# Attention in a fused kernel: 296 TensorE transposes of rounded keys and queries, issued as plain matmuls instead of in transpose mode

## Chip, core and metric

One core of one Trainium2 chip runs the whole program in one launch. The metric is the device time of that launch in microseconds (us), as the median of several runs; a profile of one further execution shows where the time goes.

## What is computed

The program chains an attention, a gated feed-forward layer and a layer of eight experts with two chosen per token. The change is in the attention alone:

```python
# q, k, v: (2, 8, 1152, 64) float32
q_pool = q.reshape(B, H, S // 2, 2, D).mean(axis=3)          # 576 pooled queries
scores = scale * np.matmul(q_pool, k.transpose(0, 1, 3, 2))  # 576 x 1152 a head
scores = scores - np.max(scores, axis=-1, keepdims=True)
attn = np.exp(scores)
attn = attn / (np.sum(attn, axis=-1, keepdims=True) + 1e-09)
out = np.matmul(attn, v)
x = out.transpose(0, 2, 1, 3).reshape(B * S // 2, H * D)     # 1152 tokens
# then: RMS norm, silu(x @ w_gate) * (x @ w_val) @ w_out; then the experts
```

## The kernel before

The attention works on two heads at a time, which makes eight pairs (`p`). Keys and pooled queries come in with tokens on the partitions. For a float32 result from TensorE's faster rounded type (F32R), each is split into a rounded part and the remainder: `khl` holds rounded keys and remainders side by side (9 chunks of 128 columns a head), `qh2` the rounded queries twice, `Ql` the queries' remainders, with the negated row maximum of the scores in one further column.

TensorE contracts over partitions, so all three are turned by transposes of 128x128 blocks: a block is the stationary operand (a weight load, engine PEld in the profile), the 128x128 unit matrix `identr` the moving one. `trans` (L131 to L143) collects up to four blocks in one PSUM bank `tt`, and ScalarE copies the bank out to `KT`, `QH` or `QlT`. `ql_trans2` (L175 to L181) does the same for four leftover blocks, one of them with a permuted unit matrix `swapr`.

For one pair there are six banks of four blocks, one of one and one of two (`kq_trans`), two banks of three (`ql_trans`) and one of four (`ql_trans2`): 37 blocks, 296 over the eight pairs.

The rest of a pair: `s1` (L188 to L191) makes scores for the row maximum, three matmuls of 384 columns a step, and VectorE reduces them (L193). `st_exp` makes the scores again, transposed and with the remainders added, by matmuls of 288 columns (L202, L203), and ScalarE takes the exponential (L204) into `et`. `avmm` (L229) multiplies `et` with the values in plain float32, and `sums` (L245) adds up the rows.

The order of the work is written out by hand: in pair `p` the lists `S_S1A`, `S_KA`, `S_QA` and so on put steps of the next pair (its transposes, most of its `s1`) between the 18 steps of `st_exp`. Every engine runs its own instructions in this order. The transposes of the first pair stand in a prologue before the loop, with those of `kq_trans` for the pairs 1 to 7 in the loop's periods 0 to 6.

A weight load can run while the matmul before it is still streaming; the load after that one has to wait until the matmul in between has started.

Of the kernel before, what the change touches and what calls it, by code (L numbers as in the profile page):

```python
# [9 lines left out]
F32 = mybir.dt.float32  # L10
F32R = mybir.dt.float32r
# [10 lines left out]
def fused_kernel(ctx, tc, q, k, v, w_gate, w_val, w_out, rms_g,  # L22
                 r_gate, r_noise, noise, e_w1, e_w2, out, dbg=None):
    nc = tc.nc
    P = 128
# [11 lines left out]
    pe, dve, act, pool, sp = nc.tensor, nc.vector, nc.scalar, nc.gpsimd, nc.sync  # L37
# [4 lines left out]
    identr = const.tile([P, P], F32R, name="identr")  # L42
# [43 lines left out]
    raw, khl, qh2, KT, QhT, QlT, V = {}, {}, {}, {}, {}, {}, {}  # L86
# [42 lines left out]
    tpool = [pst]  # L129

    def trans(srcs, evacs):  # L131
        t = tpool[0].tile([P, 512], F32R, name="tt", tag="T")
        tpool.append(tpool.pop(0))
        for i, a in enumerate(srcs):
            pe.transpose(t[:, i * P:(i + 1) * P], a, identr)
        for eng, o, lo, hi, rows in evacs:
            i = t[0:rows, lo:hi].bitcast(F32)
            if len(o.shape) == 3:
                i = i.rearrange("p (h c) -> p h c", h=2)
            if eng is act:  # L140
                act.copy(o, i)
            else:
                eng.tensor_copy(o, i)  # L143

    def kq_trans(p, h, i):
        if i == 0:
            KT[p, h] = ab.tile([P, S], F32R, name="KT", tag=f"KT{h}", bufs=NKT[h])
            qt = QH[p % 2].rearrange("p (h c) -> p h c", h=2)
            QhT[p, 0], QhT[p, 1], QhT[p] = qt[:, 0], qt[:, 1], qt
        kt = KT[p, h]  # L150
        kk = khl[p, h].rearrange("p c a d -> p c (a d)")
        qq = qh2[p, h].rearrange("p c a d -> p c (a d)")
        if i < 2:
            o = i * 512
            trans([kk[:, 4 * i + c] for c in range(4)], [(act, kt[:, o:o + 512], 0, 512, P)])
        elif i == 2:
            trans([qq[:, c] for c in range(4)], [(act, QhT[p, h][:, 0:512], 0, 512, P)])
        else:
            ev = [(act, kt[:, 1024:], 0, P, P)]
            if h == 0:  # L160
                trans([kk[:, 8]], ev)
            else:
                trans([kk[:, 8], qq[:, 4]], ev + [(act, QhT[p][:, :, QF:SQ], P, 2 * P, P),
                                                  (dve, QZ[p % 2][:, QR:], P + QR, 2 * P, P)])
# [8 lines left out]
        trans([Ql[p % 3][h][:, c] for c in range(3)], [(act, QlT[p, h][:, 0:384], 0, 384, P)])  # L173

    def ql_trans2(p):  # L175
        t = tpool[0].tile([P, 512], F32R, name="tt", tag="T")
        tpool.append(tpool.pop(0))
        for i, (a, m) in enumerate(((Ql[p % 3][0][:, 3], identr), (Ql[p % 3][1][:, 4], identr),
                                    (Ql[p % 3][1][:, 3], identr), (Ql[p % 3][1][:, 4], swapr))):
            pe.transpose(t[:, i * P:(i + 1) * P], a, m)  # L180
        act.copy(QlT[p][:, :, 384:], t.bitcast(F32).rearrange("p (h c) -> p h c", h=2)[:, :, 0:192])  # L181

    def s1(p, h, c):
        t = ps[0].tile([P, 3, 512], F32, name="s1", tag="s1", bufs=ps[1])
# [240 lines left out]
    for p in range(NPB):  # L425
# [19 lines left out]
        at(sl["s1b"][0], s1, p, 1, 3)  # L445
        at(sl["s1a"][1], s1, p, 1, 4)
        at(sl["qa"][0], ql_trans2, p)
        if p + 2 < NPB:
            if p == 0:
# [35 lines left out]
        for i in range(NST):  # L485
            g, c = divmod(i, KC)
# [1144 lines left out]
```

## Time and profile before

| | |
|---|---|
| median of 3 runs | 782.76 us (781.74 to 783.29) |
| profiled execution, its own time | 782.14 us |
| its span in the profile | 780.1 us |
| TensorE matmuls (PE) busy | 746.0 us, 96% of the span |
| weight loads (PEld) busy | 619.9 us, 79% |
| VectorE (DVE), ScalarE (ACT), GpSimd (POOL) busy | 525.2, 375.7, 258.5 us |

The attention runs until about 267 us, the feed-forward layer and the experts follow. A matmul's busy time counts its whole latency, so that overlapping matmuls can fill the PE row although TensorE waits a little in between: starts, one after another, say more than durations. PEclk, or the granted clock, is the share of full clock that the chip recorded for TensorE (1.00 is 2.4 GHz, 0.5 is 1.2 GHz).

### The profile page before, as it was taken

Reading aid. Unit: us, or ns where it says so; the run is one execution under the profiler, and the core shown is the slowest. Engines: PE = TensorE matmul, PEld = TensorE weight load, DVE = VectorE, ACT = ScalarE, POOL = GpSimd, SP = SyncE. Lnnn points to the kernel's source line nnn. Section 1 sums busy time; section 2 is a strip of 40 time slices with the busy share of each in tenths; the row PEclk is TensorE's granted clock in tenths of the full one; section 3 lists DMA queues with packets and bytes.
Section 4 is the critical chain, followed back from the end, with each engine's and each line's share of the span. In section 5 each row is a group of like instructions: output and inputs, shape, how many; then the busy total and the mean of one; then the engine's idle time right before and its main releaser. Section 6 shows DMA issues by size and latency. Waiting matters only on the chain. (4 is left out here: it accounts for less than half of the span.)

```text
span 780.1 us, 13462 instructions
## 1 busy us (share of the span) xinstructions
PE 746.0 (96%) x5102; PEld 619.9 (79%) x5102; DVE 525.2 (67%) x798; ACT 375.7 (48%) x766; POOL 258.5 (33%) x221
## 2 busy tenths in 40 slices
PE   5999999999999989999999999999999999999993
PEld 4877777877777668988888889988899898978762
DVE  6677777787779967576568654659856766748520
ACT  4665655665667553534233323355444455537510
POOL 8356365384813431122122310020323213422222
PEclk9999999999999999999999999999999999999997
DMA  7344232322041131133133201555898768879982
GB/s 224 90 134 139 83 85 53 107 77 61 27 134 63 56 108 55 55 108 108 55 108 109 57 1 55 183 180 193 280 358 258 229 186 251 271 228 361 354 263 61
DMA packets 72729, 113.29 MB, mean 145 GB/s; under 512 B 7127, under 2 KB 37551, under 8 KB 72656
## 3 DMA queue, kind: packets, MB, share of 16 engines
q1 hardware_dynamic: 67504, 101.55, 40.2%
q0 software_dynamic: 5152, 10.80, 6.3%
q8 instruction: 42, 0.69, 0.4%
q14 instruction: 31, 0.25, 0.1%
HBM read 98.16 MB, written 9.65 MB: 138 GB/s over the span
## 5 line engine op out<-in xcount | busy, mean ns | idle before, releaser
L536 PE MATMUL gv<-XN,ws 128*128 128x256 f32 (+2 forms) x912 | 165.2, 331 | 0.9 <-POOL ws L402 0.9
L536 PEld LDWEIGHTS gv<-XN,ws 128*128 128x128 f32 x912 | 143.8, 189 | 15.0 <-issue 1.8
L193 DVE TENSOR_REDUCE Ql<-s 128x1 fp32r<-128x1152 f32 x72 | 97.3, 1355 | 56.5 <-PE s L188 34.5
L204 ACT ACTIVATE et<-st 128x288 f32<-128x288 f32 x288 | 103.3, 417 | 40.9 <-PE st L203 38.6
L1086 DVE TENSOR_TENSOR wz<-raw,wz 128x1024 fp32r<-128x1024 f32 x80 | 96.0, 1222 | 28.9 <-ACT wz L106 26.4
L402 POOL TENSOR_TENSOR ws<-wm,ws 128x1024 fp32r<-128x1024 f32 x18 | 43.9, 2440 | 154.5 <-ACT ws L401 139.6
L202 PE MATMUL st<-QH,KT 128*128 128x288 f32 x288 | 91.8, 334 | 2.4 <-ACT et L204 1.0
L1187 PE MATMUL py<-wz,hTT 128*128 128x512 f32 x384 | 93.9, 395 | 0.0
L557 PE MATMUL po<-ws,hT 128*128 128x512 f32 x324 | 83.2, 395 | 2.2 <-DVE X L562 2.1
L203 PE MATMUL st<-QlT,KT 128*128 128x288 f32 x288 | 81.4, 296 | 0.0
L106 ACT CAST wz<-raw 128x1024 fp32r<-128x1024 f32 x80 | 81.1, 1047 | 0.4 <-PE py L1187 0.4
L1187 PEld LDWEIGHTS py<-wz,hTT 128*128 128x128 f32 x384 | 70.0, 188 | 13.7 <-DVE hTT L1055 0.2
L229 PE MATMUL av<-et,v 128*64 128x288 f32 x576 | 77.4, 412 | 0.5 <-ACT xT L234 0.5
L202 PEld LDWEIGHTS st<-QH,KT 128*128 128x128 f32 x288 | 54.5, 189 | 21.9 <-issue 12.3
L557 PEld LDWEIGHTS po<-ws,hT 128*128 128x128 f32 x324 | 58.9, 188 | 14.2 <-DVE X L562 3.3
L217 DVE TENSOR_TENSOR es<-es,et 128x576 f32<-128x576 f32 x64 | 62.3, 973 | 1.5
L1263 POOL DMA_INDIRECT out_dram<-yo,sidx x16 | 30.6, 1910 | 96.5 <-DVE yo L1262 55.8
L229 PEld LDWEIGHTS av<-et,v 128*64 128x64 f32 x576 | 38.3, 136 | 27.7 <-issue 3.9
L1160 PEld LDWEIGHTS ph<-xgT,wz 128*128 128x128 f32 x480 | 57.7, 189 | 0.4
L1160 PE MATMUL ph<-xgT,wz 128*128 128x256 f32 x480 | 57.8, 281 | 0.0
L203 PEld LDWEIGHTS st<-QlT,KT 128*128 128x128 f32 x288 | 54.8, 190 | 0.1
L546 ACT CAST hT<-sl 128x256 fp32r<-128x256 f32 (+2 forms) x38 | 18.9, 496 | 74.7 <-DVE sl L545 74.7
(284 smaller groups left out, 1114.4 us busy)
## 6 DMA issues: line engine op xcount, KB each, us to landing
raw<-in_moe_w_dram SPq DMA_DIRECT2D x112, 512.0 KB, 8.5
wraw<-in_moe_w_gate_dram SPq DMA_DIRECT2D x6, 1024.0 KB, 5.1
wraw<-in_moe_w_val_dram SPq DMA_DIRECT2D x6, 1024.0 KB, 5.2
wraw<-in_moe_w_out_dram SPq DMA_DIRECT2D x6, 1024.0 KB, 5.1
kraw<-in_k_dram SPq DMA_DIRECT2D x16, 288.0 KB, 3.7
v<-in_v_dram SPq DMA_DIRECT2D x8, 576.0 KB, 3.9
KT<-KT SPq DMA_DIRECT2D x16, 288.0 KB, 3.1
Qraw<-in_q_dram SPq DMA_DIRECT2D x16, 256.0 KB, 4.0
```

The costliest lines, as they stand in the source:

```text
L106: act.copy(o, i)
L193: dve.tensor_reduce(Ql[p % 3][h][:, c, D:D + 1], t[:, :, 0:384], axis=AX.XY, op=ALU.max, negate=True)
L202: pe.matmul(t[:, 0:NG], KT[p, h][:, cs], QhT[p, h][:, n0:n0 + NG], start=True, stop=False)
L203: pe.matmul(t[:, 0:NG], KT2[h][p % NKT[h]][:, cs], QlT[p, h][:, n0:n0 + NG], start=False, stop=True)
L204: act.activation(et[:, h, :], t[:, 0:NG], AF.Exp, scale=SCALE)
L217: eng.tensor_tensor(acc, acc, e, op=ALU.add)
L229: pe.matmul(av[h * D:(h + 1) * D, 0:NG], V[p][:, h, c, :], ET[p, g, c][:, h, :], start=(c == 0), stop=(c == KC - 1))
L536: pe.matmul(t[:, 0:n], w[a][:, d, j * P:(j + 1) * P], XN[hf][b_][:, d, cs], start=(k_ == 0), stop=(k_ == 11))
L557: pe.matmul(pt, HT[f, hf][a][:, j, c0:c0 + P], w[b_][:, j, :], start=(k_ == 0), stop=(k_ == 5))
L1086: eng.tensor_tensor(lo, RAW[u % 2][i], hi.bitcast(F32), op=ALU.subtract)
L1160: pe.matmul(o, w[a][:, d, j * P:j * P + P], XT[u][c][:, d], start=z + d == 0, stop=z == 2 and d == 3)
L1187: pe.matmul(PL[u, "y", k], x[c][:, f0 + d, k * P:k * P + P], w[a][:, d], start=i == 4 and z + d == 0, stop=i == 7 and z == 2 and d == 1)
```

## The change

The transposes of `trans` and `ql_trans2` lose the transpose mode: the same block stands as stationary operand, the same unit matrix streams, but as an ordinary matmul with accumulation flags. The output tile in PSUM is then declared as float32 rather than F32R, and the reinterpretations to float32 at its readers go. No instruction is added, removed or moved: each engine has the same instructions in the same order (TensorE, VectorE, ScalarE, GpSimd and the DMA queue). The float32 transposes elsewhere (L255, L285, L317, L667, L1050 and others) keep their mode.

```diff
     def trans(srcs, evacs):
-        t = tpool[0].tile([P, 512], F32R, name="tt", tag="T")
+        t = tpool[0].tile([P, 512], F32, name="tt", tag="T")
         tpool.append(tpool.pop(0))
         for i, a in enumerate(srcs):
-            pe.transpose(t[:, i * P:(i + 1) * P], a, identr)
+            pe.matmul(t[:, i * P:(i + 1) * P], a, identr, start=True, stop=True)
         for eng, o, lo, hi, rows in evacs:
-            i = t[0:rows, lo:hi].bitcast(F32)
+            i = t[0:rows, lo:hi]
...
     def ql_trans2(p):
-        t = tpool[0].tile([P, 512], F32R, name="tt", tag="T")
+        t = tpool[0].tile([P, 512], F32, name="tt", tag="T")
...
-            pe.transpose(t[:, i * P:(i + 1) * P], a, m)
-        act.copy(QlT[p][:, :, 384:], t.bitcast(F32).rearrange("p (h c) -> p h c", h=2)[:, :, 0:192])
+            pe.matmul(t[:, i * P:(i + 1) * P], a, m, start=True, stop=True)
+        act.copy(QlT[p][:, :, 384:], t.rearrange("p (h c) -> p h c", h=2)[:, :, 0:192])
```

## Rows read from the trace of the kernel before

**Rows 1.** Page, busy us and share of the span by engine.

```profile
PE 746.0 (96%) x5102; PEld 619.9 (79%) x5102; DVE 525.2 (67%) x798; ACT 375.7 (48%) x766; POOL 258.5 (33%) x221
```

**Rows 2.** Windows: stretch, length, busy by engine, granted clock, DMA share, GB/s.

```profile
20.00:24.00 4.00, 4.00 (x24) 3.96 (x22) 1.36 (x1) 2.88 (x8) 1.57 (x2) 0.57 0.78 227
...
26.00:240.00 214.00, 210.75 (x1518) 162.15 (x1518) 164.87 (x182) 130.06 (x361) 112.41 (x98) 1.00 0.30 85
...
280.00:400.00 120.00, 119.52 (x638) 104.63 (x637) 76.28 (x104) 46.32 (x79) 23.83 (x15) 0.99 0.24 79
```

**Rows 3.** Waits, 26 to 240 us: who waited for whom, us, times, longest.

```profile
ACT et L204 <- PE st L203: 33.2, 31, 2.6
...
DVE Ql L193 <- PE s L188: 28.7, 37, 1.9
...
PEld st L202 <- ACT et L204: 6.3, 20, 0.6
...
ACT KT L141 <- PE tt L135: 2.8, 7, 0.5
PEld s L188 <- DVE Ql L193: 2.0, 8, 0.3
PEld sm L245 <- ACT et L204: 1.5, 6, 0.3
ACT QlT L141 <- PE tt L135: 1.3, 6, 0.2
```

**Rows 4.** Timeline, weight loads at 62 to 66 us: start, total us, what.

```profile
62.47 0.19 PEld L202 LDWEIGHTS st<-QH,KT 128*128 128x128 f32 x1
62.57 0.19 PEld L203 LDWEIGHTS st<-QlT,KT 128*128 128x128 f32 x1
...
65.29 0.39 PEld L135 LDWEIGHTS tt<-identr,khl 128*128 128x128 f32 x4
65.63 0.19 PEld L202 LDWEIGHTS st<-QH,KT 128*128 128x128 f32 x1
65.74 0.19 PEld L203 LDWEIGHTS st<-QlT,KT 128*128 128x128 f32 x1
```

**Rows 5.** By tile and line: one load, ns min/median/max, first and last start.

```profile
L135 PEld LDWEIGHTS tt<-identr,khl x144: 137/142/228, 5.1 to 225.4; 128*128 128x128 f32 x144
...
L188 PEld LDWEIGHTS s<-KT,QH x192: 186/188/338, 8.0 to 251.3; 128*128 128x128 f32 x192
```

**Rows 6.** Timeline after 503 and 517 us: plain matmuls with few columns.

```profile
503.25 0.65 PEld L841 LDWEIGHTS tab<-ohs,oha 128*72 128x72 f32 x8
503.37 0.68 PE L841 MATMUL tab<-ohs,oha 128*72 128x128 f32 x8
...
516.96 0.97 PEld L676 LDWEIGHTS lg<-wgn,xrt 128*128 128x128 f32 x8
```

**Rows 7.** Timeline, prologue and first period, 5 to 23 us.

```profile
5.14 1.07 PEld L135 LDWEIGHTS tt<-identr,khl 128*128 128x128 f32 x8 [5.14 <-DVE khl L114]
...
8.04 1.33 PE L188 MATMUL s<-KT,QH 128*128 128x384 f32 x3 [0.55 <-ACT QH L141]
...
10.14 1.29 PE L188 MATMUL s<-KT,QH 128*128 128x384 f32 x3
...
13.28 3.89 DVE L193 TENSOR_REDUCE Ql<-s 128x1 fp32r<-128x1152 f32 x3 [0.16 <-PE s L188]
...
14.80 0.76 PE L188 MATMUL s<-KT,QH 128*128 128x384 f32 x3
...
19.33 0.40 PE L202 MATMUL st<-QH,KT 128*128 128x288 f32 x1 [0.57 <-ACT QlT L141]
...
22.78 0.29 PEld L202 LDWEIGHTS st<-QH,KT 128*128 128x128 f32 x1
...
22.95 0.33 PEld L203 LDWEIGHTS st<-QlT,KT 128*128 128x128 f32 x1
```

## The prediction

> **What bounds the kernel now.** I read the page's busy shares first: TensorE's matmuls are busy for 96% of the span, every other engine far less [rows 1]. Then the windows. In 26 to 240 us, the attention's steady part, PE is busy 210.75 of 214 us at full clock, DVE 164.87, ACT 130.06; the feed-forward stretch behind it has 119.52 of 120 us [rows 2]. So whatever delays TensorE in the attention is not made up for by a stage behind it: the next one is TensorE's own and starts later by as much.
>
> Then the waits of the attention, because busy time hides short ones. ACT's exponentials stood idle for TensorE's scores for 33.2 us in 31 places and DVE's maximum for 28.7 us in 37; TensorE's weight loads stood idle for ACT's exponentials for 6.3 us in 20, for DVE 2.0 us in 8, and for ACT before the sums 1.5 us in 6: 9.8 us in 34 places [rows 3]. The reader should see that TensorE leads, but not without slack. A delay on it passes on, except where the next thing it does is to wait for ACT or DVE anyway.
>
> Last the timeline of weight loads, since that is what this change touches.
>
> **The change, part by part.** Nothing is added, removed or moved, and the readers of the bank copy the same bytes, so their prices stay. What changes is the price of a weight load and of a matmul with 128 columns in each of 296 blocks.
>
> *The matmul.* The nearest plain F32R matmul with 128 moving columns is the table of L841: eight of them take 0.68 us; with 0.23 for the last, one starts every 0.064 us [rows 6]. That is one pass, and less than any load below, so the matmul side is costed at nothing. Its stationary operand has only 72 columns, which bears on the load, not on the stream.
>
> *The weight load.* In transpose mode four loads that start at 65.29 are followed by the next at 65.63: 0.085 us each. A plain load of 128 columns that has no long matmul to hide behind needs 0.11 us (65.63 to 65.74) or 0.10 (62.47 to 62.57) until the next one starts [rows 4]; eight plain loads before matmuls of 16 columns take 0.97 us, (0.97 - 0.19) / 7 = 0.111 each [rows 6]. I take 0.108 us, so a plain block costs 0.023 us more wherever the load is what its successor waits for. The bounds: nothing, if the load were hidden, and 0.046 us, the whole difference of the median durations, 188 against 142 ns [rows 5], if no more of it overlapped than now. I stay with 0.023, since it compares starts with starts.
>
> *How many are exposed.* The first load of a bank runs under a score matmul of 288 or 384 columns, which is longer; it stays free. From the second on, each is exposed. A bank of four has 3, of three 2, of two 1, of one none. A loop period has, from the code, 6 x 3 + 1 + 2 x 2 = 23 from the next pair's `kq_trans` and its `ql_trans`, and 3 from `ql_trans2`. Seven periods have the first, eight the second: 7 x 23 + 8 x 3 = 185. That is 185 x 0.023 = 4.3 us of TensorE time.
>
> *How much of it passes on.* Upper bound: all 4.3. Lower bound: nothing, if each bank's 0.05 to 0.07 us ended in one of the 34 waits. Against the lower bound: there are 11 banks in a period, 77 in seven, and 34 waits, and a wait swallows a delay only if its own releaser isn't delayed. But ACT and DVE stood idle for TensorE in 31 and 37 places of the same stretch, so that what releases TensorE was itself set by an earlier TensorE instruction. Against the upper one: in only 7 + 6 of these banks did ACT's copy wait for the transposes [rows 3]; mostly ACT is still busy when a bank is full, and a slightly later bank costs it nothing. I choose three quarters, nearer to all than to nothing: 3.2 us.
>
> *The prologue.* Its transposes run at the lower clock: three `s1` matmuls take 1.33 us at 8.04 and 1.29 at 10.14, but 0.76 at 14.80. A load in transpose mode takes (1.07 - 0.18) / 7 = 0.127 us there; a plain one at the lower clock 0.17 (22.78 to 22.95) [rows 7]. That is 0.04 a block. On the way to the first `s1` lie four blocks of keys, whose bank has to be copied out, and four of queries; then eight more in front of the second `s1` and six in front of the third, with the first load of each hidden: 4 + 4 + 7 + 5 = 20, or 0.8 us. At the full clock's price it would be 0.5. DVE had waited only 0.16 us for the third `s1` and then ran three reductions without a break [rows 7], so it has no slack to hide this in. I take 0.6.
>
> **The sum.** 3.2 + 0.6 = 3.8 us on the profiled execution's own 782.14 us: 785.9. That execution lies 0.6 below the median of 782.76, inside the runs' 781.74 to 783.29; by the median it would be 786.5. I say 786.2.
>
> **Rivals.**
>
> *Swallowed.* The loop's 4.3 us vanish in TensorE's waits; only the prologue's 0.6 is left: 783.4, within 0.2%, which is 1.6 us and about what a measurement of this kernel can tell from no change. For it speaks that 9.8 us of waits could hold twice the delay; against it the idle time of ACT and DVE above. Chance 0.16.
>
> *The clock rises earlier.* This one can end on the other side. Twice early on TensorE runs at the lower of its two levels (1.2 against 2.4 GHz): until about 13 us, judged by durations, and again after 20 us, where the granted clock averages 0.57 in 20 to 24 us [rows 2]. Before the first rise it did transposes and `s1` matmuls in turn, before the fall it mostly waited for DVE. If plain matmuls let the clock rise sooner, the two `s1` triples from 10.14 on come back with 1.29 - 0.76 = 0.53 us each [rows 7], 1.1 us. If the dip went too, (1 - 0.57) x 4 us = 1.7 us more. Together 2.8 us against 3.8: 783.8, no measurable change. It becomes faster by over 0.2% only if less than a seventh of the loop's 4.3 us passes on; with none of it, 782.8 + 0.6 - 2.8 = 780.6. Between the prologue's last `s1` and the dip there are only the three transposes of the second head's `ql_trans`, one at a time behind DVE, so I give little for that half. The Trainium skill (TensorE: Matmul & The Clock Gate, Part 4: PE-mode transpose) says that transposes in this mode don't count as activity for the clock gate; no row here shows it either way, because matmuls are mixed in before the rise. Chance 0.12: slower 0.05, same 0.04, faster 0.03.
>
> *Several passes.* If a plain F32R matmul with this few columns ran in four passes, 4 x 0.064 = 0.256 us would replace 0.085 in nearly every block: 296 x 0.17 = 50 us, 820 to 833 with some of it swallowed. L841's 0.064 [rows 6] speaks against it. The Trainium skill (the same page, Terms) calls trn2's transpose mode four times faster for FP32, which by itself would give this outcome; the row on rounded operands disagrees. Chance 0.04.
>
> *Loads in full.* At 0.046 us a block: 185 x 0.046 x 3/4 + 0.8 = 7.2 us, 790. Chance 0.06.
>
> **How the numbers follow.** The forecast has the remaining 0.62, nearly all of it over 1.6 us. Its own range is 785.0 (half passes on, prologue at the cheap end) to 788.0 (all 4.3 + 0.8). The range for 8 in 10 reaches down over "swallowed" and most of the clock's case to 783.0, and up to 788.4 for loads at 0.111; left out are several passes, loads in full, and faster, about 0.14. Slower: 0.60 + 0.05 + 0.04 + 0.06 = 0.75. Same: 0.02 + 0.16 + 0.04 = 0.22. Faster: 0.03.
>
> **What would show it.** Right: loads of L135 and L180 with a median near 188 ns instead of 142; four of them followed by the next after about 0.43 us instead of 0.34 where the first is not hidden; a bank's copy out unchanged; each loop period longer by 0.4 to 0.6 us, the feed-forward stretch equally long and only later; the first L202 at about 19.9 instead of 19.33 [rows 7]. Wrong: L135 matmuls 0.2 us apart (several passes); loads that stay at 142 ns (no change at all); periods of the same length with fewer waits of L202 for ACT (swallowed); the second `s1` triple in 0.8 us, or no dip after 20 us (clock).

## The result and the profile after

The change makes the kernel slower: 788.92 us median (787.37 to 789.81, 6 runs) against 782.35 (781.27 to 783.29, 6 runs), +6.6 us, ratio 1.0081 with a 95% interval of 1.0069 to 1.0093. The direction is the one forecast; the size is not: 3.8 us were predicted, and the upper end of the range was 788.4.

The busy shares of the page hardly move, and the share of the span is the same 96% ([rows 1] before):

```profile
PE 754.8 (96%) x5102; PEld 631.0 (80%) x5102; DVE 525.3 (67%) x798; ACT 378.7 (48%) x766; POOL 256.2 (33%) x221
```

The view by line has the duration of one load and one matmul (ns, least, median, most; first and last start):

```profile
L135 PEld LDWEIGHTS tt<-identr,khl x144: 186/192/338, 5.3 to 232.5; 128*128 128x128 f32 x144
L135 PE MATMUL tt<-identr,khl x144: 222/274/476, 5.3 to 232.7; 128*128 128x128 f32 x144
```

A load in `trans` now takes 192 ns where [rows 5] had 142: it has become one like those of `s1`. What a row of them costs is read from starts, in the timeline of weight loads after 66 us, which is `ql_trans2` of one pair and the scores behind it:

```profile
66.25 0.19 PEld L203 LDWEIGHTS st<-QlT,KT 128*128 128x128 f32 x1
66.38 0.43 PEld L180 LDWEIGHTS tt<-identr,Ql 128*128 128x128 f32 x3
66.73 0.19 PEld L180 LDWEIGHTS tt<-swapr,Ql 128*128 128x128 f32 x1
66.85 0.19 PEld L202 LDWEIGHTS st<-QH,KT 128*128 128x128 f32 x1
66.96 0.19 PEld L203 LDWEIGHTS st<-QlT,KT 128*128 128x128 f32 x1
```

The first load of the bank starts 0.13 us after the one before it and the second waits as long again; both follow the 288-column matmuls, as before. From there three intervals lead to 66.85: 66.38 + 0.13 = 66.51, and (66.85 - 66.51) / 3 = 0.113 us each, where transpose mode had 0.085 [rows 4]. The matmul is still one pass: two passes of 0.064 us [rows 6] would not fit between loads 0.11 us apart.

The prologue differs most. In the timeline of 5 to 26 us, to be held against [rows 7]:

```profile
5.29 1.78 PEld L135 LDWEIGHTS tt<-identr,khl 128*128 128x128 f32 x8 [5.29 <-DVE khl L114]
7.08 0.93 PEld L135 LDWEIGHTS tt<-identr,qh 128*128 128x128 f32 x4
...
8.87 1.33 PE L188 MATMUL s<-KT,QH 128*128 128x384 f32 x3 [0.46 <-ACT QH L141]
...
9.68 1.93 PEld L135 LDWEIGHTS tt<-identr,khl 128*128 128x128 f32 x8
...
11.60 1.27 PE L188 MATMUL s<-KT,QH 128*128 128x384 f32 x3
...
12.90 1.36 DVE L193 TENSOR_REDUCE Ql<-s 128x1 fp32r<-128x1152 f32 x1 [1.31 <-PE s L188]
...
13.84 2.23 PE L188 MATMUL s<-KT,QH 128*128 128x384 f32 x6
15.14 2.62 DVE L193 TENSOR_REDUCE Ql<-s 128x1 fp32r<-128x1152 f32 x2 [0.31 <-PE s L188]
...
21.85 0.61 PE L202 MATMUL st<-QH,KT 128*128 128x288 f32 x1 [0.57 <-ACT QlT L141]
...
23.72 1.27 PE L188 MATMUL s<-KT,QH 128*128 128x384 f32 x3
```

Eight loads take 1.78 us instead of 1.07, (1.78 - 0.33) / 7 = 0.21 each instead of 0.127. The first `s1` starts at 8.87 (8.04 before), the second triple of `s1` at 11.60 (10.14), the first L202 at 21.85 (19.33). Three `s1` matmuls still take 1.27 us at 23.72, so TensorE is at the lower level there; in the kernel before it had been at the higher one from about 13 to 20 us (`s1` triples of 0.76 us in [rows 7]).

Who waits for whom from 26 to 240 us is almost what it was [rows 3]. ACT and DVE wait for TensorE (31.9 and 32.1 us, before 33.2 and 28.7), TensorE for them 8.9 us instead of 9.8, so that only some 0.9 us of the new load time went into its old waits:

```profile
DVE Ql L193 <- PE s L188: 32.1, 36, 3.1
ACT et L204 <- PE st L203: 31.9, 31, 2.5
...
PEld st L202 <- ACT et L204: 6.0, 20, 0.6
...
PEld sm L245 <- ACT et L204: 1.5, 6, 0.2
...
PEld s L188 <- DVE Ql L193: 1.4, 8, 0.2
```

### The profile page after: what moved, and what is told of

It is laid out like the page before. It is cut to its first block, busy times and chain, and to the rows that moved or that the text cites. A ratio compares the mean times of both kernels' runs of the same rounds, so it can differ in the third digit from the quotient of the medians.

```text
span 787.2 us, 13462 instructions
## 1 busy us (share of the span) xinstructions
PE 754.8 (96%) x5102; PEld 631.0 (80%) x5102; DVE 525.3 (67%) x798; ACT 378.7 (48%) x766; POOL 256.2 (33%) x221
## 5 line engine op out<-in xcount | busy, mean ns | idle before, releaser
L202 PE MATMUL st<-QH,KT 128*128 128x288 f32 x288 | 91.2, 331 | 2.1 <-ACT et L204 0.8
L202 PEld LDWEIGHTS st<-QH,KT 128*128 128x128 f32 x288 | 55.0, 191 | 21.4 <-issue 12.3
```

The costliest lines, as they stand in the source:

```text
L202: pe.matmul(t[:, 0:NG], KT[p, h][:, cs], QhT[p, h][:, n0:n0 + NG], start=True, stop=False)
```

## The experiments

Two theories were told apart. **A**: the loop costs about what was forecast, and the term for the prologue, at the lower clock, is what was too small. **B**: the prologue is as forecast, and the loop costs more.

A measure that the prologue and the clock don't enter is the stretch from the first L202 of the loop's second period to that of its eighth, six periods: 239.83 - 47.37 = 192.46 us in the kernel before, 247.16 - 51.41 = 195.75 after it, from their timelines, first before, then after:

```profile
47.37 0.29 PE L202 MATMUL st<-QH,KT 128*128 128x288 f32 x1
...
239.83 0.38 PE L202 MATMUL st<-QH,KT 128*128 128x288 f32 x1
```

```profile
51.41 0.29 PE L202 MATMUL st<-QH,KT 128*128 128x288 f32 x1
...
247.16 0.38 PE L202 MATMUL st<-QH,KT 128*128 128x288 f32 x1
```

That is +3.29 us, 0.55 a period.

### The two parts apart

In the changed kernel the blocks now go through one function that chooses the mode; `loop` is empty until the prologue is done. Shown is the kernel with the plain prologue; the one with the plain loop has `if loop:` in place of `if not loop:`.

```diff
+    loop = []
+
+    def turn(o, a, m, i):
+        if not loop:
+            pe.matmul(o, a, m, start=True, stop=True)
+        else:
+            pe.transpose(o.bitcast(F32R), a, m)
...
-            pe.matmul(t[:, i * P:(i + 1) * P], a, identr, start=True, stop=True)
+            turn(t[:, i * P:(i + 1) * P], a, identr, i)
...
     tpool.remove(ps[0])
+    loop.append(1)
```

Plain in the prologue alone:

> Plain matmuls in the 33 blocks of the prologue alone, transpose mode in the 263 of the loop. Theory A (the lower clock is what was mis-sized: there a plain load takes 0.213 us and not 0.17, and TensorE stays at the lower level longer): +2.5 us until the first L202, up to 1 us more in the first period, nothing after it: 2.5 to 4.0 us over before. Theory B (the prologue costs the forecast 0.6 us, the loop is what was mis-sized): +0.6 us, no measurable change.

Measured: 784.80 us against 781.91, +2.9 us, 1.0036 (1.0024 to 1.0048). The timeline of its weight loads shows the price:

```profile
5.12 1.78 PEld L134 LDWEIGHTS tt<-identr,khl 128*128 128x128 f32 x8 [5.12 <-DVE khl L114]
...
9.51 1.93 PEld L134 LDWEIGHTS tt<-identr,khl 128*128 128x128 f32 x8
...
13.13 0.33 PEld L134 LDWEIGHTS tt<-identr,khl 128*128 128x128 f32 x1
13.34 0.33 PEld L134 LDWEIGHTS tt<-identr,qh 128*128 128x128 f32 x1
13.56 1.61 PEld L195 LDWEIGHTS s<-KT,QH 128*128 128x128 f32 x6
```

The last three of these start 0.21 us apart. The prologue costs several times the 0.6 us, as theory A has it. But in this profile, of the fastest of the six runs (783.66 us), the first L202 stands at 21.07 us, +1.74 and not the +2.5 of theory A, and the second period starts 1.87 us late: the slower clock that A counted on beside the loads isn't seen in it.

Plain in the loop alone:

> The other part alone: transpose mode in the prologue, plain in the loop. Theory A: about 0.55 us in each of seven periods, 3.3 to 4.2 us over before, with the first L202 where it was (19.3). Theory B: 5.5 to 6.5 us. The two runs should add up to the 6.6 us of the whole change, within a microsecond.

Measured: 785.95 us, +4.0 us, 1.0052 (1.0038 to 1.0065). Its first L202 stands at 19.07 us, close to where it was (19.33). Six periods take 195.80 us, +3.34:

```profile
49.16 0.29 PE L209 MATMUL st<-QH,KT 128*128 128x288 f32 x1
...
244.96 0.38 PE L209 MATMUL st<-QH,KT 128*128 128x288 f32 x1
```

The profile is of the slowest of the five runs (787.55 us): its first period, 49.16 - 19.07 = 30.09 us against 47.37 - 19.33 = 28.04 in the kernel before, holds 2.0 us more and not 0.55, with a longer stretch at the lower level (below, "What stays open"). The two parts add up to 6.9 us against 6.6 for the whole. Theory B falls.

### Which blocks of the loop cost

In the loop, plain for the first block of each bank (`if loop and i == 0`), and for the others (`if loop and i > 0`):

> Plain only for the first block of each bank in the loop (78 of 263), whose load hides behind a score matmul of 288 or 384 columns. If only exposed loads cost, the periods stay at the 30.8 us of before (within 0.05 us each), and the time is the one of before. If every plain block costs the same, 78/263 of the loop's loss: 0.16 us a period, 1.2 us in all.

> The complement: plain only for the second to fourth block of each bank in the loop (185 of 263). If only exposed loads cost, the whole 0.55 us a period of the plain loop; if every block costs the same, 0.39 us.

Measured: the first blocks 782.73 us against 782.38, 1.0001 (0.9991 to 1.0010), no change; the others 786.41, +4.0 us, 1.0049 (1.0033 to 1.0064). Second and eighth period, first the kernel with plain first blocks, then the other:

```profile
48.25 0.29 PE L209 MATMUL st<-QH,KT 128*128 128x288 f32 x1
...
240.95 0.38 PE L209 MATMUL st<-QH,KT 128*128 128x288 f32 x1
```

```profile
48.76 0.29 PE L209 MATMUL st<-QH,KT 128*128 128x288 f32 x1
...
244.32 0.38 PE L209 MATMUL st<-QH,KT 128*128 128x288 f32 x1
```

Six periods take 192.70 and 195.56 us, 0.04 and 0.52 a period more than before. A load that runs under a long matmul costs next to nothing more when it is plain (0.04 us a period for eleven of them); the loop's loss comes from those that don't.

### Plain from the second period on

```diff
     for p in range(NPB):
         F = [[] for _ in range(2 * NST)]
+        if p == 1:
+            loop.append(1)
```

with `if len(loop) > 1` in `turn`.

> Plain only from the second period of the loop on, transpose mode in the prologue and the first period. Theory A (the loop's steady price, 0.555 us a period, and nothing else): 6 x 0.555 = 3.3 us over before. The plain loop as a whole had 4.0; the difference is then the first period's. Theory B (the first period, which runs at the lower clock for part of its time, holds more than its 0.555 us): the second period starts where before has it, within the clock's half microsecond or so, the time is at most 3.5 us over before.

Measured: 785.86 us against 782.25, +3.6 us, 1.0045 (1.0031 to 1.0059). In its profile the second period starts at 47.60 us and the eighth at 243.46, six periods in 195.86, +3.40:

```profile
47.60 0.29 PE L209 MATMUL st<-QH,KT 128*128 128x288 f32 x1
...
243.46 0.38 PE L209 MATMUL st<-QH,KT 128*128 128x288 f32 x1
```

So the first period holds some 0.4 of the loop's 4.0 us by the medians. Each of the two is known to about 1.1 us only, so this agrees with a share of 0.55, as theory A has it; theory B of this run, that the first period holds more, isn't borne out, but isn't excluded either.

### The clock

Small matmuls in front, where TensorE is idle until 5.1 us, with the whole change and with the kernel before:

```diff
+    hot = const.tile([P, 256], BF16, name="hot")
+    dve.memset(hot, 1.0)
...
+    ht = pst.tile([P, 512], F32, name="ht", tag="T")
+    for i in range(18):
+        pe.matmul(ht[:, 0:256], hot[:, 0:P], hot, start=True, stop=True)
```

> The whole change, with 18 bf16 matmuls of 256 columns on a constant put in front of the first transpose, where TensorE is idle until 5.1 us; their result is not read. If they bring the clock up before or soon after the first transposes: theory A expects the prologue's loss down to about 0.5 us, so 2 to 4 us faster than the changed kernel. Theory B: the loss stays in the loop, and only what the higher clock gives to all, 1 us or so.

> The kernel before with the same 18 matmuls in front. Theory A: faster than before by 1 to 2.8 us (the price of the two low stretches of its first 24 us), and the distance to the run of the whole change with these matmuls is 4.0 to 4.8 us (loop 3.8 and 20 exposed loads at 0.026) instead of 6.6. Theory B: the distance stays 6 us or more.

Measured: 789.26 us with the change, 1.0092 (1.0076 to 1.0107), and 781.90 without, 0.9996 (0.9987 to 1.0005). Neither gained by the median, so this expectation of theory A failed, and the distance of the two, 7.4 us, is where theory B had it (6 us or more). The windows show when the clock was low (the number behind the GpSimd column is the granted clock), first with the change, then without:

```profile
13.00:20.00 7.00, 4.26 (x19) 3.38 (x18) 4.68 (x10) 1.68 (x4) 6.51 (x9) 0.74 0.72 161
20.00:24.00 4.00, 3.98 (x18) 3.75 (x18) 1.36 (x1) 2.30 (x7) 1.53 (x2) 0.60 0.82 237
```

```profile
0.00:13.00 13.00, 10.90 (x58) 8.27 (x59) 6.42 (x15) 6.92 (x13) 9.49 (x17) 0.87 0.84 242
13.00:20.00 7.00, 3.88 (x22) 2.87 (x20) 5.42 (x10) 1.64 (x4) 6.60 (x9) 0.93 0.71 173
20.00:24.00 4.00, 3.92 (x23) 3.67 (x22) 1.36 (x1) 2.86 (x8) 2.19 (x3) 0.69 0.62 170
```

The clock came up early, but was taken back later: 2 x (0.26 x 7 + 0.40 x 4) = 6.8 us at the lower level with the change, before the loop had found its pace. From 13.0 to 16.4 us, ahead of that fall, TensorE was busy for 2.11 of 3.4 us and waited for DVE in between.

The profile with the change is of the fastest of its four runs, 787.58 us; the others, at 789.25 to 789.32, have none. In it the prologue did gain: its first two `s1` triples run at the higher level,

```profile
8.36 0.79 PE L190 MATMUL s<-KT,QH 128*128 128x384 f32 x3 [0.52 <-ACT QH L143]
...
9.83 0.73 PE L190 MATMUL s<-KT,QH 128*128 128x384 f32 x3
```

the second period starts at 47.89 us, 3.5 before that of the changed kernel and 0.9 after that of the other warmed one (46.97), and at the eighth (243.71 against 239.35) the distance is 4.4 us, within the 4.0 to 4.8 of theory A. The rest, 1.9 us, is lost behind the attention, where TensorE was also low for longer (granted clock 0.57 in 282 to 290 us, against 0.79 in 278 to 286 in the other). Why the other three runs are slower is not shown.

So the next two kernels keep TensorE busy in these waits as well: small matmuls in front, behind the first head's banks, and between the transposes that wait for DVE, there in columns of the bank that nothing reads. `heat(n, o)` issues `n` of them; the numbers given to `ql_trans` say how many stand before each of its transposes.

```diff
+    heat(36, ht[:, 0, 0:P])
...
     for i in range(4):
         kq_trans(0, 0, i)
+        heat((0, 3, 0, 8)[i], ht[:, 0, 0:P])
...
-            ql_trans(0, 0)
+            ql_trans(0, 0, (0, 0, 8))
-    ql_trans(0, 1)
+    ql_trans(0, 1, (2, 7, 14))
```

> The whole change, with small bf16 matmuls on a constant wherever TensorE would wait in the first 19 us (36 in front, 11 behind the first head's banks, 31 between the transposes that wait for DVE), so that the clock comes up early and is not withdrawn before the loop. Their result is not read. Theory A (clock): the loss against the next run is the loop's 6 x 0.555 + 0.55 = 3.9 us and about 0.5 in the prologue, 4.4 us, in place of 6.6. Theory B (all of the loss is the weight loads, whatever the clock): 6 us or more.

> The kernel before with the same small matmuls. Theory A: the low stretch of 3.4 us around 20 us is gone and the prologue runs at the full clock: 1 to 2.5 us faster than before. Warming the front alone gave nothing (1.00), since the low stretch came anyway; if it comes again here, the result is again no change.

Measured: 784.72 us with the change, 1.0028 (1.0018 to 1.0037), and 779.88 without, 0.9965 (0.9952 to 0.9979). The latter is faster than both kernels of this case, by 2.5 us (782.38 beside it) and 9.0 (788.92). Its windows have no low stretch, and the second triple of `s1` takes 0.76 us at 9.12:

```profile
15.00:20.00 5.00, 3.83 (x41) 3.41 (x41) 2.84 (x9) 1.68 (x4) 4.79 (x5) 1.00 0.54 140
20.00:24.00 4.00, 3.88 (x30) 3.56 (x28) 1.63 (x2) 3.32 (x10) 1.59 (x2) 1.00 0.78 224
...
9.12 0.76 PE L192 MATMUL s<-KT,QH 128*128 128x384 f32 x3
```

The distance of the two is 4.8 us instead of 6.6, 0.4 more than theory A had. In the profile with the change the clock came up later, between its first two triples of `s1`, when part of the prologue was done; in its timeline of matmuls:

```profile
9.15 1.31 PE L192 MATMUL s<-KT,QH 128*128 128x384 f32 x3
...
11.18 0.74 PE L192 MATMUL s<-KT,QH 128*128 128x384 f32 x3
```

Keeping the clock up takes back some of the loss; the loop's share stays: six periods take 242.25 - 46.51 = 195.74 us against 237.46 - 45.02 = 192.44, +3.30 as before.

### The same kernels a second time

> The kernel before once more, for a second profile. Theory A (the steps in which the clock comes and goes fall differently on the program from execution to execution): the first L202 and the start of the second period move by up to 2 us against the first profile, periods from the second on keep their 30.8 us. Theory B (the kernel alone sets the clock): rise near 13.3 us and a low stretch of 3.4 us from 20.1 again, everything within 0.2 us.

> The changed kernel once more. Theory A: the third step of s1 starts 1.7 to 1.9 us later than in the kernel before, as far as TensorE runs low until then, since loads are 0.213 us apart there; the clock may now rise before 27 us, and the second period then begins 2.5 to 3.5 us later instead of 4.0. Theory B: low until 27.2 again, 4.0.

> Plain blocks in the prologue alone, once more: the first profile had the clock of the kernel before and +1.9 us at the second period, while the median was +2.9. Theory A: a longer or second low stretch this time or none, so that the second period starts anywhere between +1 and +3.5; Theory B: +1.9 again.

Each is one execution, taken for its profile (781.97, 788.94 and 784.08 us). The windows of 20 to 28 us, in this order:

```profile
20.00:24.00 4.00, 4.00 (x25) 3.97 (x24) 1.36 (x1) 3.19 (x8) 1.79 (x3) 0.60 0.72 214
24.00:28.00 4.00, 4.00 (x28) 3.64 (x27) 2.02 (x2) 3.36 (x10) 0.00 (x0) 0.98 0.42 127
```

```profile
20.00:24.00 4.00, 3.22 (x12) 3.03 (x13) 1.09 (x7) 1.88 (x4) 1.71 (x3) 0.50 0.75 217
24.00:28.00 4.00, 4.00 (x23) 3.88 (x22) 1.36 (x1) 2.59 (x7) 0.00 (x0) 0.70 0.22 87
```

```profile
20.00:24.00 4.00, 2.72 (x12) 2.56 (x13) 1.64 (x7) 1.86 (x4) 2.27 (x3) 0.65 0.59 178
24.00:28.00 4.00, 3.86 (x27) 3.63 (x26) 1.36 (x1) 3.04 (x9) 0.00 (x0) 0.92 0.34 126
```

From their timelines: the kernel before starts its second period at 47.39 us (47.37 the first time); the changed kernel at 50.83 (51.41), with the third triple of `s1` at 13.70 (13.84); the plain prologue at 49.81 (49.24). So the loads' price repeats: counted from the first transpose, the third triple stands 1.74 us later in both profiles of the changed kernel (13.84 - 5.29 and 13.70 - 5.15, against 11.95 - 5.14 before) and 1.73 in the first of the plain prologue (13.66 - 5.12). The clock adds something to the start of the second period that differs from execution to execution: about 0.1 and 0.6 us in the plain prologue, 1.6 and 1.2 in the changed kernel (whose first period also holds 0.55 of loads). For the kernel before, theory B of that run was nearer: its low stretch moved by only 0.6 us, to no effect. For the other two, theory A held: +3.5 us at the second period for the changed kernel, low until 26.4 us, and +2.4 for the plain prologue.

## Why the direction was right and the size wrong

*The matmul at nothing.* Right: one pass, as L841 had it; "several passes" would have been 50 us.

*The load, 0.023 us a block.* Nearly right: 0.113 - 0.085 = 0.028 us by the banks shown, 0.026 with the 0.111 of L676; the row of L676 at 0.111 was the better neighbour than the 0.108 that was taken. "Loads in full" (0.046) is refuted.

*185 exposed loads.* Right, and shown: plain first blocks cost 0.04 us a period, the others 0.52, all of them 0.55.

*Three quarters pass on.* A little low. 26 x 0.026 = 0.68 us of load time a period, with 0.111 for a load, became 0.55, so four fifths; over seven periods 0.9 us are missing, as much as TensorE's waits lost (9.8 to 8.9 us). The loop has 4.0 us by the median where 3.2 were predicted. "Swallowed" is refuted.

*The prologue.* This is the step that failed: "a plain one at the lower clock 0.17", hence "0.04 a block" and "I take 0.6". A row of plain loads at the lower clock has 0.21 us from start to start, so a block costs 0.213 - 0.127 = 0.086, and the 20 blocks on the way to the third triple of `s1` 1.7 us. The trace has that triple 1.89 us later (13.84 against 11.95), 0.15 of it because the first block starts later (5.29 against 5.14), and DVE, with no slack, passes it on.

```profile
11.95 1.29 PE L188 MATMUL s<-KT,QH 128*128 128x384 f32 x3
```

The count of 20 was right: with the same 0.15 taken off, the three triples stand 0.68, 1.31 and 1.74 us later, steps of 0.68, 0.63 and 0.43 for 8, 7 and 5 blocks, 0.09 each. The 0.17 had been read between two loads behind a transpose [rows 7]. It is the first interval of a row, which is shorter: of the 1.78 us of the plain prologue's first eight loads the last takes 0.33, and six intervals at 0.213 (13.13, 13.34 and 13.56 are 0.21 and 0.22 apart) take 1.28, which leaves 0.17 for the first. One interval was taken for the rate. In the whole the prologue costs 2.9 us by the median (interval 1.9 to 3.8), where 0.6 were predicted; 1.7 of it are loads.

By the medians the two parts cost 4.0 + 2.9 = 6.9 us against 3.2 + 0.6 = 3.8, and 6.6 measured. By loads alone it would be 1.74 + 7 x 0.55 = 5.6 us, 1.1 more than forecast in the prologue and 0.7 in the loop, and a kernel at the median of before would take 788.0, still within the range. The last 1.0 us is no load time. By the medians alone it could be chance (the interval of the 6.6 reaches down to 5.4), but both profiles of the changed kernel have it. The sum held no term for it, since it let the clock of the kernel before stand, and its rival let the clock rise only earlier.

*The clock.* The rival said that plain matmuls might bring it up earlier. No run shows that: in the kernel before, the `s1` triple at 14.80 us takes 0.76; in the two profiles of the plain prologue the matching one takes 0.74 at 16.55, and the six matmuls from 16.78 still 1.79, where six at the higher level take 1.55 in the kernel before that is kept warm. (The Trainium skill, TensorE: Matmul & The Clock Gate, Part 4: PE-mode transpose, which says that such transposes don't count as busy, finds no support in these runs, and none decides it.) But the clock did take part, on the other side. The changed kernel's second period starts 4.0 and 3.5 us late in its two profiles; the prologue's loads made 1.74 of that, a loop period 0.55, and a later first block 0.15 in the first, which leaves 1.6 and 1.2 us. In them TensorE is at the lower level until 27.2 and 26.4 us, against about 23.5 and 24.2 in the kernel before.

*What stays open.* Whether plain blocks in the first period make the low stretch longer. Worked out from the granted clock of the windows, it lasted about 6.9 us in the profiles with plain blocks there and a transpose-mode prologue (the plain loop, its later blocks alone, its first blocks alone), and about 3.4 in those with transposes there. But in the former it also happened to begin earlier against the first L202, when TensorE was still waiting, and that could do the same. One profile speaks against this: in the second of the plain prologue, with transposes in the first period, the stretch began at about 21.2 us, before the first L202 (21.61), and still lasted 3.4. What the longer stretch costs isn't settled either: the profile with plain first blocks has it, and starts its second period 0.9 us late, but it is the slowest of ten runs whose median is that of the kernel before. The later-periods run puts the first period's part at 0.4 us, with either median known to 1.1 us. So the 1.0 us that is no load time lies before the second period and goes with a longer time at the lower level; that the one causes the other, and why it lasts longer, stays open.

## What to carry to other kernels

A block transposed as an ordinary matmul is still one pass, but has a slower weight load: price it by the interval between loads in a row of several, at each clock level apart, and only where no long matmul lies over the load. Two instructions in a row give a first interval, not a rate. A few microseconds at a kernel's start, where TensorE runs at the lower level, can weigh as much as a small loss repeated through a long loop; filling TensorE's waits there with small matmuls whose result nothing reads was worth 2.5 us here in the kernel before and 4.2 in the changed one (784.72 against 788.92), filling only the time before its first instruction nothing by the median.

## What the runs showed of the hardware

- A plain F32R load of 128 columns repeats every 0.111 us at the higher level and every 0.213 at the lower, twice as long; in transpose mode 0.085 and 0.127, which is only half as long again. Transpose mode therefore saves 0.026 us a load at one level and 0.086 at the other.
- In the first profiles of the kernel before and of the changed kernel the granted clock reads 1.00 over 0 to 13 us, although three `s1` matmuls take 1.33 us at 8.04 and 8.87, and in the changed kernel's also over 20 to 24 and 24 to 28 us, while three `s1` matmuls take 1.27 us at 23.72 instead of 0.76. Durations tell the level there, the clock column doesn't.
